# GateLoop attention and a maxout FFN on one core: the weights' conversion in four computing steps, joined output sums, constant biases, and new order lists

## The chip, the cores and the metric

The kernel runs on one core of one Trainium2 chip. The metric is the time of one execution on the device in microseconds (us). The engines are TensorE (PE in the profile, with its weight loads as PEld), VectorE (DVE), ScalarE (ACT), GpSimd (POOL) and SyncE (SP), which here only issues transfers. Each engine works off its own instructions in order.

## The reference

```python
batch, n_heads, seq, head_dim = (4, 8, 768, 48)           # q, k, v, a_re, a_im: float32
n_tokens, d_model, d_ff = (3072, 384, 768)                # w1, w2, w3, w_out: float64

mag = np.sqrt(a_re * a_re + a_im * a_im)
scale = np.minimum(mag, 0.999) / (mag + 1e-06)
a_re_n, a_im_n = (a_re * scale, a_im * scale)
for t in range(S):
    ar, ai = (a_re_n[:, :, t, :, None], a_im_n[:, :, t, :, None])
    new_re = ar * S_re - ai * S_im
    new_im = ar * S_im + ai * S_re
    kv = np.einsum('bhd,bhe->bhde', k[:, :, t], v[:, :, t])
    S_re, S_im = (new_re + kv, new_im)
    y[:, :, t] = np.einsum('bhd,bhde->bhe', q[:, :, t], S_re)
# y as (B*S, H*D) is x
h = np.maximum(np.maximum(x @ w1, x @ w2), x @ w3)
return (h @ w_out).astype(np.float32)
```

A linear recurrence whose state decays and turns by a complex gate at every step gives y; y is the input of a feed-forward layer that takes the largest of three products and multiplies it by a fourth matrix. The four weight matrices come as float64.

## The kernel before, in words

**Stages.** The 4 x 768 tokens are worked off in 12 groups g = 0 to 11, each of 128 positions of two batch rows, x and y. For each group the attention part works in chunks of 64 positions, and the feed-forward part takes the group's 256 tokens. Several groups are under way at once.

**Lists written out by hand.** `SCHEDULE` is one long list of words such as `Qcx:0`: a step's name (here with the batch row x) and its group. `run` issues the instructions of each word in the list's order, and the class `Bound` chains those of each engine, so that every engine keeps the list's order; waits between engines follow from the data. (All instructions pass through `Bound`, so the profile gives line 210 for nearly all of them and they are told apart by tiles.) `SLOTS` names, for each PSUM tile in order, which of four double banks it takes. `OTHER` names the words that run on another engine than the usual one: copies and magnitudes go to DVE in place of ACT, additions made by an accumulating transfer of POOL's queue go to DVE as an add.

**The steps.**

- `Lr`, `Li`, `Lk`, `Lq`, `Lv` load a_re, a_im, k, q, v on SP's queue; k, q and v with four transfers a word.
- Gates, on 128 x 768 tiles (two halves, `0` and `1`, in group 0): `sqr`, `sqi` (ACT squares), `add` (DVE), `lnL`, `expw`, `expe`, `relu`, `lne` (ACT), `Lnop` (adds lne's result to relu's, a transfer from group 1 on unless in `OTHER`), `abs`, `pw` or `addw` (a sum on PE, or from group 2 on an adding transfer or, in `OTHER`, DVE), `lnw`, `expL`, `mulai`, `mulw`, `stt`, `xor`, `half`, `atan`, `turn`. They end in the log magnitude `Ln` and the angle `w`.
- Angles: `cs` (running sums on PE), `t`, `nf`, `af`, `sa`, `sb` (sines), and `Cd`, a small adding transfer on POOL's queue that carries the last angle into the next group.
- Decays: `sums` and `F` (PE), `En`, `Ek`, `Eq`, `f0` to `f3` (ACT exponentials), `mk`, `mq`, `uk`, `uq`, `kEn` (DVE products).
- Scores: `tpk`, `tpq` (PE transposes), copies `Kc`, `Qc`; factors `Q1`, `Q2`, `KB`, `QB`, `QG` (DVE); `A`, `B` (PE) and picks into the masked tile: `g0` to `g3` (DVE), `b0`, `b1` (ACT).
- State and output: `dk` (PE), `h0` to `h3` (DVE); `y` (PE), copy `x`.
- Feed-forward: `U01`, `U11`, `U02`, `U12` (PE, 18 matmul instructions each) with `u..` (maximum with zero or with the other); sums `S1` to `S4` (DVE); products `P1` to `P7`, `Px`, `Py` (PE, a seven-product scheme); `r1` (ACT), `r6`, `r5`, `r7`, `r57`, `ox`, `oy` (DVE); stores `Dx`, `Dy` on SP's queue. Group 0 has forms of its own (`U..x`, `u..x`, `O`, `o`), six matmuls to each half product.

**The weights.** Twelve blocks i of doubles, 128 x 768 a block and 768 KB each, are loaded raw (`WLi`) and turned into float32 bit by bit: `Wa` (ACT) takes the high words, one in two, as floats, drops the sign and scales by 2^-112; `Wb` (DVE) limits; `Wc` (DVE) shifts left by 3; `We` (DVE) puts in the top bits of the low words; `Wf` (DVE) puts in the sign and writes the block. Blocks 0, 3 and 6 get the opposite sign. `Wg` adds the negated w1 to w2 or w3. `T`, `t`, `M`, `m` form the product of w1 and w_out, and `J` the differences of w_out that the seven products need. A raw block lies in a room that is free at that time (`ROOMS`).

**Set of functions.** `activation` loads ACT's table when a word's function belongs to another set than the loaded one; functions outside `SETS` count as being in every set.

**Tiles.** Tiles with two buffers come from pools (`ldx`, `nat2`, `un2`, `fp2`); `Ek` and `Eq` share the two buffers of tag `E`, `t` and `af` those of tag `t`.

Of the kernel before, what the change touches and what calls it, by code (L numbers as in the profile page):

```python
# [26 lines left out]
turn1:0 Lry:1 sqr:1 t1:0 WL11:0 Lkx:0 tx:0 nfx:0 Wa11:0 Wb10:0 csy:0 afx:0 sax:0 mkx:0 Wb11:0 Wc10:0 Lix:1 sbx:0
uqx:0 sqi:1 Lix:2 Wc11:0 Lky:0 tpqx:0 ty:0 add:1 f3x:0 f2x:0 ukx:0 Fy:0 Qcx:0 We10:0 Wf10:0 nfy:0 tpkx:0 We11:0
lnL:1 WL2:0 Q2x:0 kEnx:0 Eqy:0 expe:1 Eky:0 relu:1 xor:1 expw:1 QBx:0 Kcx:0 abs:1 T2:0 T0:0 t0:0 CL:0 KBx:0 WL1:0
Wa1:0 pw:1 Q1x:0 mky:0 Wb1:0 f0y:0 f1y:0 Wc1:0 t2:0 f2y:0 Wf11:0 lne:1 Lnop:1 Ax:0 g0x:0 Lry:2 g1x:0 We1:0 g2x:0  # L30
half:1 Lqy:0 Cdx:0 f3y:0 Liy:2 Lvx:0 mqy:0 Wa2:0 Wb2:0 lnw:1 expL:1 M0:0 mulw:1 Wc2:0 M1:0 mulai:1 dkx:0 Wf1:0
# [5 lines left out]
Wb7:0 Wg4:0 U11x:0 xor:2 By:0 dky:0 U02x:0 Lvx:1 b1y:0 h1y:0 b0y:0 QGy:0 yy:0 addw:2 lnw:2 expL:2 xy:0 U11y:0 Wg5:0
u02x:0 U02y:0 afx:1 half:2 u11x:0 Wc7:0 lne:2 We7:0 mulw:2 mulai:2 sbx:1 h2y:0 Z4:0 sax:1 h3y:0 stt:2 atan:2 Wf7:0
U12x:0 u12x:0 say:1 sby:1 Cdy:1 WL8:0 Cdx:1 turn:2 ukx:1 uqx:1 U01y:0 u01y:0 u11y:0 Wa8:0 U12y:0 csy:2 ty:2 u12y:0
csx:2 tpqx:1 tx:2 u02y:0 Qcx:1 nfy:2 Lnop:2 nfx:2 tpkx:1 Fy:1 kEnx:1 Wb8:0 Wc8:0 We8:0 Kcx:1 Wg7:0 Wf8:0 U21y:0  # L40
Wg8:0 KBx:1 f0y:1 u21y:0 Lky:1 Lqy:1 mky:1 afy:2 sumsx:2 dkx:1 Q1x:1 f1y:1 f2y:1 f3y:1 Enx:2 U21x:0 u21x:0 afx:2
U22y:0 u22y:0 Oy:0 Lqx:2 mqy:1 uky:1 uqy:1 tpqy:1 Ekx:2 Lix:3 Q2x:1 say:2 sby:2 sbx:2 sax:2 Eqx:2 h0x:1 h1x:1 QGx:1
h2x:1 oy:0 QBx:1 mkx:2 h3x:1 Qcy:1 Q1y:1 tpky:1 Kcy:1 Ax:1 g0x:1 Q2y:1 Liy:3 sqi:3 Fx:2 sumsy:2 g1x:1 g2x:1 U22x:0
Lrx:3 u22x:0 g3x:1 f3x:2 f2x:2 f1x:2 f0x:2 Lry:3 sqr:3 add:3 lnL:3 expe:3 Ay:1 relu:3 J3:0 g0y:1 g1y:1 mqx:2 g2y:1
Bx:1 KBy:1 kEny:1 lne:3 Ox:0 Eky:2 b1x:1 Eny:2 QBy:1 b0x:1 h0y:1 ukx:2 By:1 Eqy:2 yx:1 g3y:1 xx:1 b1y:1 Lqy:2 mqy:2
Lvx:2 ox:0 Lky:2 mky:2 b0y:1 tpkx:2 expw:3 Kcx:2 uqx:2 Lnop:3 uqy:2 tpqx:2 Qcx:2 QGy:1 dky:1 h1y:1 kEnx:2 sumsx:3
# [5 lines left out]
xx:2 By:2 u02:1 Ay:2 S1:1 nfy:3 relu:4 tx:3 expe:4 S2:1 expw:4 P5:1 P6:1 g0y:2 afy:3 say:3 sby:3 nfx:3 sbx:3 g1y:2
afx:3 sax:3 abs:4 dky:2 P1:1 Lqy:3 g2y:2 g3y:2 b1y:2 J4:0 QGy:2 P7:1 Px:1 P2:1 b0y:2 h0y:2 h1y:2 ukx:3 tpkx:3 lne:4
Lnop:4 r1:1 Liy:5 mky:3 h2y:2 h3y:2 S4:1 Kcx:3 uqx:3 yy:2 Lqx:4 kEnx:3 mqy:3 tpqx:3 Qcx:3 P3:1 r6:1 xy:2 Py:1 r5:1
r7:1 P4:1 Fy:3 uky:3 r57:1 f0y:3 f1y:3 xor:4 half:4 oy:1 ox:1 Q1x:3 addw:4 dkx:3 h1x:3 Lvy:3 f2y:3 f3y:3 h0y:3
h2x:3 sumsx:4 Ekx:4 h3x:3 lnw:4 QGx:3 expL:4 Eqx:4 Fx:4 KBx:3 U11:2 Dx:1 QBx:3 mulai:4 Q2x:3 f2x:4 Enx:4 u11:2
Cdy:3 Lkx:4 f1x:4 f0x:4 U01:2 uqy:3 f3x:4 mulw:4 stt:4 atan:4 tpky:3 Kcy:3 Ax:3 g0x:3 mqx:4 g1x:3 Bx:3 g2x:3 g3x:3
b1x:3 b0x:3 u01:2 Cdx:3 turn:4 U02:2 Lrx:5 u02:2 mkx:4 kEny:3 csy:4 csx:4 tx:4 nfx:4 ty:4 nfy:4 yx:3 xx:3 sumsy:4
KBy:3 Eqy:4 Eky:4 Lry:5 S3:2 Eny:4 sqr:5 dky:3 h1y:3 h2y:3 h3y:3 tpqy:3 Qcy:3 Q2y:3 Lix:5 sqi:5 Px:2 afy:4 add:5
lnL:5 expe:5 Dy:1 U12:2 u12:2 S1:2 Py:2 P7:2 Q1y:3 relu:5 lne:5 QBy:3 afx:4 P4:2 Ay:3 By:3 expw:5 S2:2 g0y:3 sbx:4  # L60
abs:5 g1y:3 sax:4 QGy:3 ukx:4 uqx:4 P6:2 P5:2 S4:2 g2y:3 g3y:3 P2:2 P1:2 Lqy:4 r1:2 Liy:6 mqy:4 b1y:3 P3:2 b0y:3
r6:2 r5:2 r7:2 tpkx:4 r57:2 ox:2 oy:2 kEnx:4 tpqx:4 yy:3 xy:3 Fy:4 say:4 Lky:4 sby:4 mky:4 uky:4 Lnop:5 Kcx:4 uqy:4
sumsx:5 xor:5 half:5 U11:3 KBx:4 addw:5 lnw:5 expL:5 mulw:5 Lqx:5 mulai:5 Cdx:4 h0x:4 f2y:4 stt:5 f3y:4 Ekx:5 f0y:4
Lkx:5 Dy:2 Dx:2 Qcx:4 Enx:5 Q1x:4 Cdy:4 u11:3 Eqx:5 QBx:4 mkx:5 Lry:6 QGx:4 Lvx:4 U01:3 Lix:6 atan:5 Q2x:4 u01:3
f1y:4 h0y:4 U02:3 Lrx:6 u02:3 sqr:6 dkx:4 h1x:4 sqi:6 h2x:4 h3x:4 Fx:5 f0x:5 f3x:5 add:6 f1x:5 f2x:5 Ax:4 g0x:4
Lqy:5 g1x:4 Bx:4 lnL:6 expe:6 g2x:4 g3x:4 U12:3 lne:6 b1x:4 tpky:4 turn:5 mqx:5 b0x:4 tpqy:4 Qcy:4 u12:3 Lvy:4
# [5 lines left out]
f1y:5 lnw:6 Lqx:6 h0y:5 u11:4 Q2x:5 expL:6 mulai:6 mulw:6 U01:4 u01:4 tpky:5 h0x:5 Eqx:6 Kcy:5 tpqy:5 stt:6 Ax:5
Lix:7 atan:6 g0x:5 Qcy:5 g1x:5 g2x:5 Bx:5 kEny:5 g3x:5 b0x:5 Q2y:5 U02:4 sqi:7 b1x:5 add:7 lnL:7 relu:7 expe:7
u02:4 U12:4 Fx:6 f2x:6 S3:4 f3x:6 half:6 turn:6 f0x:6 u12:4 Lvy:5 dky:5 h1y:5 Q1y:5 f1x:6 sumsy:6 dkx:5 Eny:6 csy:6
csx:6 h1x:5 mqx:6 S1:4 Dy:3 ty:6 nfy:6 S2:4 Eqy:6 Lqy:6 mqy:6 Eky:6 P1:4 KBy:5 tx:6 nfx:6 afx:6 lne:7 expw:7 afy:6
P7:4 abs:7 Lky:6 Ay:5 QBy:5 g0y:5 g1y:5 g2y:5 yx:5 g3y:5 addw:7 sbx:6 sax:6 ukx:6 uqx:6 By:5 say:6 P5:4 xx:5 P6:4
r1:4 r6:4 r5:4 lnw:7 xor:7 S4:4 half:7 Px:4 P2:4 b0y:5 Py:4 r7:4 P4:4 r57:4 P3:4 expL:7 mulw:7 QGy:5 oy:4 tpqx:6
tpkx:6 b1y:5 Lnop:7 mky:6 Qcx:6 Q1x:6 ox:4 Liy:8 kEnx:6 yy:5 sumsx:7 xy:5 Cdx:6 Enx:7 Fy:6 f2y:6 f0y:6 f3y:6
mulai:7 f1y:6 Eqx:7 QBx:6 QGx:6 Q2x:6 stt:7 Lqx:7 Ekx:7 Lix:8 U01:5 sqi:8 Lry:8 Cdy:6 Kcx:6 Lrx:8 Lvx:6 dkx:6 h1x:6
sby:6 mqx:7 h2x:6 h3x:6 uqy:6 uky:6 sqr:8 add:8 Dy:4 atan:7 turn:7 Ax:6 g0x:6 lnL:8 Lkx:7 expe:8 xor:8 g1x:6 relu:8  # L80
# [962 lines left out]
```

## Time and profile before

| | before |
|---|---|
| runs | 560.33, 556.86, 561.97 us; median 560.33 |
| profiled execution: span | 556.9 us, equal to the run of 556.86 |
| PE busy | 524.6 us (94%) |
| DVE busy | 490.4 us (88%), 770 instructions |
| ACT busy | 370.0 us (66%), 652 instructions |
| POOL busy | 74.4 us (13%) |
| DMA | 49.09 MB, mean 88 GB/s |

The span runs from the first to the last instruction. Busy time is the union of an engine's instructions; a matmul's end is modelled, and neighbours overlap. Rows of a view by groups read: line, engine, operation, out<-in by tile names, shape, count, then busy us, mean ns of one, and idle time before with what ended it.

### The profile page before, as it was taken

Reading aid. Unit: us, or ns where it says so; the run is one execution under the profiler, and the core shown is the slowest. Engines: PE = TensorE matmul, PEld = TensorE weight load, DVE = VectorE, ACT = ScalarE, POOL = GpSimd, SP = SyncE. Lnnn points to the kernel's source line nnn. Section 1 sums busy time; section 2 is a strip of 40 time slices with the busy share of each in tenths; the row PEclk is TensorE's granted clock in tenths of the full one; section 3 lists DMA queues with packets and bytes.
Section 4 is the critical chain, followed back from the end, with each engine's and each line's share of the span. In section 5 each row is a group of like instructions: output and inputs, shape, how many; then the busy total and the mean of one; then the engine's idle time right before and its main releaser. Section 6 shows DMA issues by size and latency. Waiting matters only on the chain.

```text
span 556.9 us, 22739 instructions
## 1 busy us (share of the span) xinstructions
PE 524.6 (94%) x10086; PEld 449.0 (81%) x10086; DVE 490.4 (88%) x770; ACT 370.0 (66%) x652; POOL 74.4 (13%) x117
## 2 busy tenths in 40 slices
PE   1669799989999999999999999999999999999997
...
DVE  5999999989998899999988897999999999886524
...
GB/s 218 287 191 156 206 154 102 78 105 123 18 108 109 21 123 77 48 63 92 68 115 82 33 61 121 110 88 50 58 126 31 32 88 82 10 31 2 7 25 29
DMA packets 142530, 49.09 MB, mean 88 GB/s; under 512 B 130528, under 2 KB 135648, under 8 KB 142432
## 3 DMA queue, kind: packets, MB, share of 16 engines
...
q14 instruction: 19, 0.16, 0.1%
...
## 4 chain that ended last, share of the span: by engine, by line
PE 84%; DVE 6%; DMA 4%; SPq 2%; issue 1%; ACT 1%; POOL 0%; DVEq 0%
PE up L210 34%; PE op L210 24%; PE y L210 7%; PE A L210 5%; PE tp L210 4%; PE dk L210 4%; PE sums L210 3%; PE cs L210 2%; SPq L210 2%; DMA xhx<-in_moe_w_out_dram 2%; PE F L210 2%; DVE xhx L210 1%; PE B L210 1%; DMA k<-in_k_dram 1%; DMA ar<-nf 1%
## 5 line engine op out<-in xcount | busy, mean ns | idle before, releaser
L210 PE MATMUL up<-xhx,w 128*128 128x256 f32 x792 | 177.4, 382 | 0.1
L210 PEld LDWEIGHTS up<-xhx,w 128*128 128x128 f32 x792 | 148.6, 190 | 21.5 <-PE B L210 0.3
L210 ACT ACT_TABLE_LOAD x45 | 57.7, 1283 | 1.5 <-PEq L1027 0.8
L210 ACT COPY atm<-B 32x128 f32<-32x128 f32 x96 | 24.5, 255 | 36.9 <-DVE atm L210 22.9
L210 PE MATMUL op<-wo,xhx 128*128 128x192 f32 (+1 forms) x220 | 48.5, 364 | 0.0
L210 DVE TENSOR_TENSOR Q<-Q,f 112x1024 f32<-112x1024 f32 (+1 forms) x48 | 45.4, 950 | 0.8 <-ACT Q L210 0.6
L210 ACT ACTIVATE f<-F 48x232 f32<-48x232 f32 x96 | 34.4, 359 | 13.2 <-PE F L210 5.4
L210 POOL DMA_DIRECT2D ar<-nf x40 | 34.2, 1280 | 65.3 <-DVE ar L210 54.7
L210 PE MATMUL y<-atm,vb 128*32 128x64 f32 x1152 | 39.4, 221 | 1.4 <-issue 1.1
L210 PEld LDWEIGHTS op<-wo,xhx 128*128 128x128 f32 x220 | 36.5, 190 | 4.3 <-DVE q L210 0.3
L210 POOL DMA_DIRECT2D Ln<-e x11 | 11.1, 1005 | 214.6 <-ACT e L210 53.9
L210 PE MATMUL y<-QG,g 112*32 112x64 f32 x1408 | 38.4, 219 | 0.9 <-issue 0.8
L210 PEld LDWEIGHTS y<-atm,vb 128*32 128x32 f32 x1152 | 32.5, 109 | 6.4 <-issue 3.6
L210 PEld LDWEIGHTS y<-QG,g 112*32 112x32 f32 x1408 | 34.8, 109 | 1.3 <-issue 1.0
L210 DVE TENSOR_TENSOR ot<-ot,op 128x192 f32<-128x192 f32 (+1 forms) x67 | 27.1, 413 | 9.0 <-PE op L210 4.3
L210 PE MATMUL op<-wo,strassen 128*128 128x192 f32 x176 | 33.0, 331 | 0.0
L210 PE MATMUL A<-Q,K 112*32 112x80 f32 x1536 | 31.6, 234 | 1.3 <-DVE Q L210 1.3
L210 DVE COPY_PREDICATED atm<-masko,A 128x256 f32<-128x256 uint8 x72 | 31.2, 435 | 1.6
L210 PE MATMUL op<-w,strassen 128*128 128x192 f32 x176 | 32.5, 329 | 0.0
L210 PEld LDWEIGHTS A<-Q,K 112*32 112x32 f32 x1536 | 27.2, 110 | 5.0 <-issue 1.9
L210 ACT COPY Q<-tp 112x1024 f32<-112x1024 f32 x23 | 23.3, 1013 | 10.3 <-PE tp L210 10.0
L210 ACT COPY ot<-op 128x192 f32<-128x192 f32 (+1 forms) x13 | 4.5, 342 | 38.2 <-PE op L210 38.2
...
## 6 DMA issues: line engine op xcount, KB each, us to landing
...
```

The lines of the kernel that those rows point to most:

```text
L210: ins = f(*a, **kw)
```

## The change

1. Conversion: `Wb` comes first, reads the high words from the raw block and limits them on both sides; `Wa` takes its result with a parametric rectifier, whose slope for negative inputs sets the bits that the shift turns into the sign; `Wf` is gone, and `We` writes the block.
2. Joined sums: `r5` and `r7` become one instruction `r75` over both halves, with the shared operand read twice.
3. Constant biases: three bias columns in SBUF become immediate numbers.
4. Tiles: the pools `ldx`, `nat2`, `un2`, `fp2` give way to fixed pairs, taken by c (x or y) or g; `Ek`, `Eq` and `En` have a pair each, `t` and `af` share one; `ot` is one tile for both rows.
5. `SCHEDULE`, `SLOTS` and `OTHER` are new throughout. The old list has 190 changes of PE's tile shape from step to step, the new one 187; 12 additions (`Lnop`, `addw`, `Wg8`) are in the new `OTHER`, 2 in the old.

```diff
-Lrx:0 Lix:0 sqi0:0 WL0:0 sqr0:0 xor0:0 add0:0 Wa0:0 Wb0:0 Wc0:0 We0:0 Liy:0 Wf0:0 lnL0:0 expw0:0 expe0:0 relu0:0
-lne0:0 Lnop0:0 Zf:0 Lry:0 sqi1:0 xor1:0 sqr1:0 WL3:0 abs0:0 add1:0 Wa3:0 half0:0 Wb3:0 Wc3:0 lnL1:0 expe1:0 expw1:0
-We3:0 lne1:0 relu1:0 Lnop1:0 Wf3:0 pw0:0 lnw0:0 expL0:0 mulai0:0 abs1:0 Lrx:1 half1:0 WL6:0 mulw0:0 Liy:1 Wa6:0
...
+Lrx:0 sqr0:0 Lix:0 sqi0:0 add0:0 lnL0:0 expe0:0 expw0:0 relu0:0 WL0:0 Wb0:0 lne0:0 Lry:0 sqr1:0 Wa0:0 Liy:0 Zf:0 sqi1:0
+Lry:1 WL3:0 Lqy:0 WL6:0 Lkx:0 WL9:0 Lix:1 WL10:0 Lqx:0 Lrx:1 Liy:1 Lnop0:0 abs0:0 Fx:0 sumsx:0 pw0:0 add1:0 Wc0:0 xor0:0
+Wb3:0 lnL1:0 f0x:0 expe1:0 expw1:0 relu1:0 lne1:0 Wa3:0 We0:0 Lnop1:0 half0:0 Wc3:0 Wb6:0 We3:0 xor1:0 f1x:0 abs1:0
...
-Zf:0 Zg:0 Wg8:0 xx:2 relu:4 afy:3 Kcy:3 xx:3 relu:5 xy:3 afx:5 addw:6 u01:4 afx:6 afy:6 abs:7 relu:8 Kcy:6 afy:7
-afx:7 relu:9 abs:9 u11:7 u01:7 afx:9 Kcx:9 xy:8 u11:8 Kcy:9 afy:10 abs:11 Kcx:10 Qcy:10 Kcy:11 Kcx:11 xy:11 u01:11
-u11:11
+Zf:0 Zg:0 afx:0 relu:1 Qcy:0 addw:2 Lnop:2 Wg8:0 u21y:0 xx:1 addw:3 relu:4 afy:3 afx:3 abs:4 Lnop:4 Kcx:3 u01:2 xx:3
+afy:4 afx:4 Qcx:4 u01:3 Kcy:4 xx:4 relu:6 xy:4 addw:6 u11:4 relu:7 afy:6 abs:7 addw:7 Lnop:7 u11:5 Lnop:8 Kcy:6 Qcy:6
+afx:7 Kcx:7 afy:8 Lnop:9 Qcx:8 xy:7 u01:7 afy:9 Qcx:9 xx:9 relu:11 afx:10 xy:9 Lnop:11 Kcx:10 addw:11 u01:9 Qcx:11
+Kcy:11 Qcy:11 Kcx:11 xx:11 xy:11 u11:11
...
-    LAST = float(np.array(0x0FEFFFFF, dtype=np.int32).view(np.float32))
+    LAST = float(np.array(0x47EFFFFF, dtype=np.int32).view(np.float32))
...
-    biases = const.tile([P, 4], FP, name="biases")
-    for i, b in enumerate((-0.5 * math.pi, LNMAX, math.exp(-LNMAX))):
-        dve.memset(biases[:, i:i + 1], b)
-    hpi, lnmax, least = (biases[:, i:i + 1] for i in range(3))
+    biases = const.tile([P, 1], FP, name="biases")
+    dve.memset(biases, 1.0)
...
+    kqs = {nm: two_of(nm, 2, 4, D) for nm in "kq"}
+    turned = {nm: two_of(nm, DM) for nm in ("t", "nf")}
+    css = two_of("CS", H, 2, D)
+    lns = two_of("Ln", W)
+    es = {nm: two_of(nm, DM) for nm in ("Ek", "Eq", "En")}
+    Ks, Qs = two_of("K", H, P), two_of("Q", 4 * H, 80)
+    ots = const.tile([P, C, DM], FP, name="ot")
...
-        if step == "a":
-            activation(out=ex.bitcast(FP), in_=high.bitcast(FP), func=AF.Abs, scale=2.0 ** -112)
-        elif step == "b":
-            dve.tensor_single_scalar(out=ex.bitcast(FP), in_=ex.bitcast(FP), scalar=LAST, op=OP.min)
+        if step == "b":
+            dve.tensor_scalar(out=ex.bitcast(FP), in0=high.bitcast(FP), scalar1=LAST, scalar2=-LAST, op0=OP.min,
+                              op1=OP.max)
+        elif step == "a":
+            activation(out=ex.bitcast(FP), in_=ex.bitcast(FP), func=AF.Prelu, alpha=-2.0 ** 32,
+                       scale=-2.0 ** -112 if i in (0, 3, 6) else 2.0 ** -112)
         elif step == "c":
-            if i in (0, 3, 6):
-                dve.tensor_scalar(out=ex, in0=ex, scalar1=3, scalar2=-0x80000000, op0=OP.logical_shift_left,
-                                  op1=OP.bitwise_or)
-            else:
-                dve.tensor_single_scalar(out=ex, in_=ex, scalar=3, op=OP.logical_shift_left)
+            dve.tensor_single_scalar(out=ex, in_=ex, scalar=3, op=OP.logical_shift_left)
         elif step == "e":
-            dve.scalar_tensor_tensor(out=ex, in0=low, scalar=29, in1=ex, op0=OP.logical_shift_right, op1=OP.bitwise_or)
-        elif step == "f":
-            dve.scalar_tensor_tensor(out=dst.bitcast(I32), in0=high, scalar=-0x80000000, in1=ex,
-                                     op0=OP.bitwise_and, op1=OP.bitwise_xor)
+            dve.scalar_tensor_tensor(out=dst.bitcast(I32), in0=low, scalar=29, in1=ex, op0=OP.logical_shift_right,
+                                     op1=OP.bitwise_or)
...
-                activation(out=e, in_=e, func=AF.Ln, scale=1e-6 * math.exp(-LNMAX), bias=least)
+                activation(out=e, in_=e, func=AF.Ln, scale=1e-6 * math.exp(-LNMAX), bias=math.exp(-LNMAX))
...
+                if name == "r75":
+                    two_ = ot.rearrange("p c n -> p (c n)")[:, NH:3 * NH].rearrange("p (u n) -> p u n", u=2)
+                    again = yl.rearrange("p (u n) -> p u n", u=1).to_broadcast([P, 2, NH])
+                    dve.tensor_tensor(out=two_, in0=again, in1=ps[:, 1, 0:DM].rearrange("p (u n) -> p u n", u=2), op=OP.add)
+                    return
```

More of the change, by code (lines that the diff above doesn't have):

```diff
@@ L27 @@
[L27 to L31, printed above, removed]
@@ L37 @@
[L37 to L41, printed above, removed]
@@ L42 @@
[L42 to L46, printed above, removed]
@@ L52 @@
[L52 to L56, printed above, removed]
@@ L57 @@
[L57 to L66, printed above, removed]
@@ L72 @@
[L72 to L80, printed above, removed]
-g2x:6 mkx:7 U11:5 KBx:6 u11:5 g3x:6 U12:5 u01:5 lne:8 U02:5 u12:5 S3:5 Lnop:8 u02:5 Bx:6 b0x:6 b1x:6 tpky:6 tpqy:6
@@ new lines @@
+Eqy:2 By:1 Ox:0 h1y:1 J3:0 Eky:2 b1y:1 lnL:3 relu:3 Eny:2 expe:3 expw:3 b0y:1 xor:3 mkx:2 uqx:2 ukx:2 h2y:1 QGy:1 mky:2
+uky:2 ox:0 abs:3 tpqx:2 tpkx:2 h3y:1 kEnx:2 addw:3 yy:1 Kcx:2 Qcx:2 xy:1 dkx:2 Fy:2 Q2x:2 Q1x:2 mqy:2 h0x:2 h1x:2 f0y:2
+f1y:2 f3y:2 lne:3 f2y:2 lnw:3 expL:3 uqy:2 QBx:2 half:3 U11:1 u11:1 J1:0 KBx:2 mulw:3 Lnop:3 tpky:2 tpqy:2 Ax:2 Kcy:2
+Qcy:2 Lvy:2 Liy:4 Lvy:3 Lry:4 Lrx:4 Lvx:3 Lqx:3 Lqy:3 Dx:0 U01:1 g0x:2 g1x:2 Q1y:2 g2x:2 g3x:2 h2x:2 Q2y:2 kEny:2 h3x:2
+Cdx:2 Cdy:2 sumsy:3 Bx:2 u01:1 Ay:2 Fx:3 h0y:2 mulai:3 g0y:2 g1y:2 b1x:2 b0x:2 sqr:4 Eny:3 g2y:2 stt:3 KBy:2 atan:3
@@ new lines @@
+Eky:3 g3y:2 U12:1 U02:1 QGx:2 sqi:4 Eqy:3 f1x:3 f0x:3 f3x:3 f2x:3 yx:2 QBy:2 u12:1 turn:3 add:4 J2:0 lnL:4 u02:1 S1:1
+xor:4 csx:3 csy:3 xx:2 tx:3 relu:4 nfx:3 sumsx:3 dky:2 ty:3 S2:1 Enx:3 expw:4 By:2 Ekx:3 Eqx:3 b1y:2 nfy:3 afx:3 h1y:2
+h2y:2 h3y:2 QGy:2 S3:1 P5:1 P6:1 Px:1 P1:1 P7:1 afy:3 expe:4 abs:4 say:3 sbx:3 b0y:2 sax:3 sby:3 r1:1 J4:0 addw:4 lne:4
+Dy:0 Lix:5 Lrx:5 Lry:5 Lkx:3 Liy:5 mqx:3 half:4 Cdx:3 S4:1 P2:1 P3:1 Py:1 yy:2 xy:2 uqx:3 r6:1 mkx:3 r75:1 ukx:3 mqy:3
+h0x:3 uqy:3 r57:1 tpkx:3 tpqy:3 tpqx:3 Lky:3 Kcx:3 kEnx:3 P4:1 Qcy:3 lnw:4 Qcx:3 Fy:3 dkx:3 expL:4 oy:1 Lnop:4 mky:3
```

202 lines of the change are left out of this document (112 added, 90 removed).

## The prediction

> **What bounds the kernel now.** I read four views in this order: the page, the table of busy time by stretches, the chain that ended last in order of time, and the groups of instructions by form. The page first: span, busy time, slices.
>
> ```profile
> span 556.9 us, 22739 instructions
> PE 524.6 (94%) x10086; PEld 449.0 (81%) x10086; DVE 490.4 (88%) x770; ACT 370.0 (66%) x652; POOL 74.4 (13%) x117
> PE   1669799989999999999999999999999999999997
> DVE  5999999989998899999988897999999999886524
> ```
>
> PE looks like the bound, but its first eight slices are loose while DVE is full from the second on. So I cut the span where it changes hands: at 9.38 (DVE begins to run without rest), 74.54 (step yy:0 starts on PE), 117.36 (yy:1 starts). The columns are stretch, length, then busy time and count of PE, PEld, DVE, ACT, POOL, the clock, DMA share and GB/s.
>
> ```profile
> 9.38:74.54 65.16, 49.36 (x762) 32.72 (x762) 64.58 (x100) 61.38 (x109) 21.00 (x31) 0.90 0.89 212
> 74.54:117.36 42.82, 41.48 (x881) 33.41 (x880) 41.78 (x66) 36.74 (x66) 6.40 (x7) 1.00 0.58 105
> 117.36:556.90 439.54, 433.76 (x8447) 382.83 (x8444) 381.11 (x594) 267.81 (x471) 40.01 (x48) 1.00 0.35 66
> 100.00:180.00 80.00, 78.36 (x1788) 66.25 (x1790) 76.16 (x120) 56.31 (x103) 10.04 (x12) 1.00 0.51 94
> 300.00:500.00 200.00, 199.86 (x4069) 176.35 (x4068) 184.13 (x287) 127.81 (x232) 19.99 (x24) 1.00 0.35 67
> ```
>
> DVE is busy 64.6 of 65.2 us and then 41.8 of 42.8; after 117.36 PE is busy 433.8 of 439.5. The time is therefore **DVE's list up to about yy:1, then PE's list to the end**. The chain agrees: DVE pieces up to 74, PE pieces behind (start, length, what).
>
> ```profile
> 61.89 0.95 DVE L L210
> ...
> 73.58 0.86 DVE ai L210
> 75.09 1.15 PE y L210 x64
> 76.80 7.12 PE up L210 x60
> ...
> 126.08 1.04 PE tp L210 x28
> ...
> 132.36 1.24 PE A L210 x64
> 133.90 4.08 PE up L210 x18
> 137.98 1.73 PE y L210 x112
> 143.79 1.45 PE cs L210 x16
> 149.57 1.07 PE dk L210 x57
> ...
> 164.17 7.97 PE up L210 x36
> 204.31 11.85 PE up L210 x54
> ```
>
> These give PE's price of each step: U 3.98 (one alone 4.08, two 7.97, three 11.85), y 1.73, A 1.24, a pair tpk and tpq 1.04, a pair cs 1.45, dk 1.0, and so on. Summed along the old list they give 434.5 us of PE work from yy:1 to the end; the table above has 433.8 busy there.
>
> **The change, part by part.** Durations of the operations that come, go or move:
>
> ```profile
> L210 DVE SCALAR_TENSOR_TENSOR w<-w,xhx 128x768 int32<-128x768 int32 x3 | 2.9, 952 | 0.0
> L210 DVE SCALAR_TENSOR_TENSOR w<-w,ai 128x768 f32<-128x768 f32 x11 | 10.5, 952 | 0.1
> L210 DVE TENSOR_SCALAR xhx<-xhx 128x768 f32<-128x768 f32 x12 | 7.5, 621 | 2.8 <-ACT xhx L210 2.7
> L210 ACT ACTIVATE xhx<-w 128x768 f32<-128x768 f32 x4 | 3.6, 912 | 2.5 <-DMA w<-in_moe_w_dram 2.5
> L210 DVE TENSOR_TENSOR w<-w,L 128x768 f32<-128x768 f32 x11 | 10.5, 951 | 0.0
> L210 POOL DMA_DIRECT2D Ln<-e x11 | 11.1, 1005 | 214.6 <-ACT e L210 53.9 <-DVE QB L210 50.8 <-ACT xhx L210 34.8
> L210 DVE COPY Q<-tp 112x1024 f32<-112x1024 f32 x1 | 1.2, 1225 | 0.5 <-PE tp L210 0.5
> L210 DVE TENSOR_SCALAR Ln<-L 128x768 f32<-128x768 f32 x4 | 2.2, 551 | 0.0
> L210 DVE TENSOR_TENSOR ot<-ot,op 128x192 f32<-128x192 f32 x46 | 16.1, 351 | 5.9 <-ACT ot L210 3.7 <-PE op L210 1.3
> L210 DVE TENSOR_TENSOR ot<-ot,op 128x384 f32<-128x384 f32 x21 | 11.1, 549 | 3.1 <-PE op L210 3.0
> L210 ACT ACTIVATE e<-e,biases 128x768 f32<-128x768 f32 x7 | 6.6, 938 | 0.0
> L210 ACT ACTIVATE e<-e 128x768 f32<-128x768 f32 x4 | 3.4, 844 | 0.1
> L210 ACT ACT_TABLE_LOAD x45 | 57.7, 1283 | 1.5 <-PEq L1027 0.8
> ```
>
> On a full DVE neighbours overlap, as two starts 0.47 us apart show at a duration of 0.55:
>
> ```profile
> 28.19 0.55 DVE L210 SCALAR_TENSOR_TENSOR nf<-t,cs 128x384 f32<-128x384 f32 x1
> 28.66 0.55 DVE L210 TENSOR_SCALAR xhx<-xhx 128x768 f32<-128x768 f32 x1
> ```
>
> So I charge each DVE instruction its duration less 0.075.
>
> *Conversion.* Step f is gone: 12 x (0.952 - 0.075) = 10.5 us off DVE, every one ahead of yy:1. Step b now reads the high words out of the raw doubles, every second word, instead of a dense tile. The trace has no one-source DVE instruction on such an input. Lower bound 0.55 (28.66 above; the mean of 621 holds a few lengthened ones), so nothing is lost; upper bound the 0.952 of the full-length instructions, +0.40 each, +4.8 in all. I take the lower: step f's row reads that same alternate word at 952 ns, just like the dense `w<-w,ai` at 952, so the gap in the input costs nothing there. [...] Step a's ACT work goes from strided (912) to dense (844), 12 x 0.07 = 0.8 off ACT.
>
> *Joined sums.* r5 and r7 (2 x 0.276) become one r75 of 384 columns (0.474): 11 x 0.08 = 0.9 off DVE in late stages, where PE covers it: nothing.
>
> *Constant biases.* 938 against 844: 0.09 off some 40 ACT instructions, 3.8 us; ACT rests 72 of the 200 us from 300 on, so nothing there.
>
> *Adding transfers and other moved steps.* Ten more adds go from POOL's queue to DVE (2 before, 12 now, weights' Wg8 in both), 10 x 0.88 = 8.8 us. Ahead of yy:1 the new list has addw:2 and Lnop:2 (0.88 each), relu:1 (0.48), afx:0 (0.28), Qcy:0 (1.15), xx:1 (0.48), u21y:0 (0.34) new on DVE: together 4.5. Behind yy:1 the new list has 384.5 us of DVE work for 370.2, 14.3 more, with copies of K, Q and x among it; DVE rests 58 of those 440 us, so I book it at nothing, and without that cover it costs up to 14 us. What was queued behind these adds on POOL, the carry transfers Cd, gets free earlier. Each Lnop on DVE now stops DVE until ACT's lne is done; behind it stand products and picks for A, y and dk.
>
> *Lists and tiles.* Fixed tiles keep the same two buffers, and Ek and Eq no longer share theirs; nothing. Changes of PE's tile shape fall from 190 to 187; two U together take 7.97 against 2 x 4.08, so a change costs 0.19 and three save 0.6. On SP the q and k loads of stage 0 now stand ahead of some weight blocks, and DVE itself, no longer ACT, waits for a block to land.
>
> *Sum.* Ahead of yy:1 the old list has 104.7 us of DVE work. It ended at 117.3 (116.74 and 0.55, the sum into the carried state that yy:1 needs), since DVE began late and rested a little:
>
> ```profile
> 115.05 1.22 DVE L210 TENSOR_TENSOR QG<-Q,f 112x1024 f32<-112x1024 f32 x1
> 116.74 0.55 DVE L210 TENSOR_TENSOR g<-g,dk 112x384 f32<-112x384 f32 x1 [0.48 <-PE dk L210]
> ```
>
> The new list has 104.7 - 10.5 + 4.5 - 0.5 (some moved past) = 98.2 behind QGy:1, the last that yy:1 needs: -6.5. PE's rest is 435.2, +0.7. The tile changes give -0.6, mostly inside that rest already, so I count none. DVE's first conversion step starts 0.9 earlier, as it needn't wait for step a. Against that stands ACT: in the old list ACT's work ahead of mulai0 (9.0) equals DVE's (9.1); in the new one it is 11.0 against 7.9. DVE will wait for ACT in the first 35 us; bounds 0 and the whole 3.1, I take half, 1.5. By yy:1 that makes 556.9 - 6.5 + 0.7 - 0.9 + 1.5 = 551.7, with the 5 us of PE waits behind yy:1 (439.5 less 434.5) kept. In the new order an earlier step is later: Oy:0 needs u22y:0, with 80.0 us of DVE work ahead of it and 455.3 of PE from Oy:0 on, 535.3 together, where yy:1 has 533.4. The old list's u22y:0 ended 12.1 after the work ahead of it:
>
> ```profile
> 93.30 0.42 DVE L210 TENSOR_TENSOR hT<-hT,up 128x256 f32<-128x256 f32 x1 [0.16 <-PE up L210]
> ```
>
> (93.7 for 81.6.) 80.0 + 12.1 + 455.3 + 5.0 - 0.9 + 1.5 = **553.0**, for an execution like the profiled one.
>
> The profiled execution is the fastest of the three shown (556.86, 560.33, 561.97); the median lies 3.4 higher, and nothing in one trace says how far the new kernel's median will lie above its best, from 0 to 3.4. Fewer landings of adding transfers are waited for, so I add 1.0: **554.0**, 1.1% under the median.
>
> **Rivals.**
>
> *The head stays as long* (ACT or a landing bounds it, or step b runs at 0.95). For it: ACT is busy 61.4 of 65.2, so DVE's relief soon meets it; DVE's step b stands in front of everything while blocks land. Against: the alternate-word rows. Price: +4.8 for step b, or the 6.5 not gained: 558 to 559.5, with the median's 1.0 some 559.5.
>
> *More falls away.* The 5 us of waits behind yy:1 shrink too, and ACT isn't met: 553.0 - 4 - 1.5 = 547.5. For it: 300 to 500 shows PE idle just 0.14 us, so an order with almost no waits exists.
>
> *DVE starves PE in stages 1 to 5 (slower).* Place: 100 to 180, where DVE rests 3.8 of 80 us and stages 3 and 4 bring it two of the adds, three copies of K or Q and other moved steps, net 6 us; Lnop holds DVE until lne, with the picks for y behind it. It decides (slower by 1%) once PE's idle time behind yy:1 exceeds 5 + 3.9 + 5.6 = 14.5 us. If each of the ten adds lets PE wait 1.5 us: 553 + 15 = 568. Against: DVE work ahead plus PE work behind is 533.6 at dkx:3 and 527.7 at Ax:5, under the head's 535.3.
>
> *The new activation function isn't in ACT's loaded table.* Two loads around each of 12 steps a, 24 x 1.28 = 31 us of ACT, nearly full there: at least 575. Against: 45 loads are exactly the list's 44 changes of set and the first, so the fillers (absolute value, copy) cause none. [...]
>
> **How the numbers follow.** Forecast 0.50 (own range 549 to 558, four fifths of it at least 1% faster); head as long 0.20; more falls away 0.10; starved 0.14; tables 0.06. One per cent (5.6 us, about what a measurement here can tell) sets the bounds 554.7 and 565.9. Faster: 0.40 + 0.10 = 0.50. Slower: 0.14 + 0.06, and 0.02 from the tail of the second case: 0.22. Same: 0.10 + 0.18 = 0.28. The range runs from 545 to 564; it leaves out the tables and most of the starved case.
>
> **What would show it.** Right: DVE full from 8.5 us; step b at 0.55; yy:1 starting at 111 to 114; PE idle about 5 us behind it; 49 table loads (the new list has four more changes of set, 5 us of ACT). Wrong: step b near 0.9, DVE gaps put down to ACT or landings in the first 40 us above 5 us, or PE idle of over 10 us between 115 and 300.

## The result: 565.7 us, 1.0% slower, and the profile after

The changed kernel takes 565.68 us (median of four runs, 564.95 to 567.12); the kernel before, run beside it on the same chip, 560.81. The ratio is 1.010, with a 95% interval of 1.006 to 1.014. The forecast was 554.0, 1.1% faster.

The page of the changed kernel (span, busy times, then the 40 slices of PE, DVE and of the granted clock):

```profile
span 565.0 us, 22654 instructions
PE 527.3 (93%) x10086; PEld 449.6 (80%) x10086; DVE 495.2 (88%) x769; ACT 359.5 (64%) x642; POOL 65.0 (12%) x107
PE   3669689999999999999999999999999999999997
DVE  3899999999999999989989898999999999797423
PEclk9779999999999999999999999999999999999999
```

The span is 8.1 us longer than before's 556.9; the medians differ by 4.9, since the profiled executions are single ones: before's was a good one, this one (567.12) is the slowest of its four.

First the arithmetic, in groups by form of the changed kernel (step b on two of its kinds of block, step a, step c, and the table loads):

```profile
L202 DVE TENSOR_SCALAR xhx<-w 128x768 f32<-128x768 f32 x4 | 2.5, 613 | 4.5 <-DMA w<-in_moe_w_dram 4.5
L202 DVE TENSOR_SCALAR xhx<-strassen 128x768 f32<-128x768 f32 x3 | 1.7, 555 | 0.0
L202 ACT ACTIVATE xhx<-xhx 128x768 f32<-128x768 f32 x12 | 10.1, 841 | 4.4 <-DVE xhx L202 4.3
L202 DVE TENSOR_SCALAR xhx<-xhx 128x768 int32<-128x768 int32 x12 | 9.1, 756 | 0.0
L202 ACT ACT_TABLE_LOAD x49 | 62.9, 1283 | 1.6 <-PEq L1028 0.8
```

Step b takes 0.55 to 0.61 us on alternate words, as on a dense tile (0.55 and 0.62 in the kernel before); step f is gone; the new function costs no table load beyond the list's own (49 loads). Behind the bars stands what is new: 4.5 us of DVE idle before step b, for a landing, and 4.3 of ACT before step a, for DVE.

The busy times by stretches, of the kernel before (first four rows) and of the changed one (columns as in the prediction):

```profile
10.00:20.00 10.00, 7.80 (x68) 3.45 (x72) 9.63 (x18) 9.25 (x20) 6.37 (x13) 1.00 1.09 335
40.00:60.00 20.00, 19.35 (x283) 12.19 (x282) 19.93 (x30) 18.92 (x28) 10.40 (x13) 1.00 0.79 169
60.00:80.00 20.00, 16.12 (x415) 13.78 (x416) 19.86 (x32) 18.06 (x37) 7.54 (x9) 1.00 0.89 182
80.00:100.00 20.00, 19.89 (x286) 16.27 (x285) 19.57 (x30) 17.74 (x32) 1.63 (x2) 1.00 0.55 91
```

```profile
10.00:20.00 10.00, 7.12 (x62) 3.96 (x58) 5.74 (x11) 7.93 (x19) 5.24 (x14) 1.00 0.95 262
40.00:60.00 20.00, 16.09 (x172) 9.49 (x171) 19.93 (x29) 17.05 (x29) 9.15 (x13) 1.00 0.90 197
80.00:100.00 20.00, 19.76 (x370) 16.71 (x371) 19.32 (x34) 15.96 (x29) 1.12 (x2) 1.00 0.57 97
118.22:565.00 446.78, 437.11 (x8464) 382.75 (x8460) 389.88 (x599) 261.48 (x466) 34.59 (x41) 1.00 0.29 58
```

DVE is busy 5.7 us of 10 to 20 where it was 9.6; PE then gets 16.1 us of work in 40 to 60 instead of 19.4. From yy:1 (118.22) to the end PE rests 9.7 us, where it rested 5.8; none of that lies right behind yy:1 (up to 180 us PE rests 0.1 of 61.8). DVE's waits in the first 120 us (total, times, longest; first the two long ones of the kernel before, then those of the changed one), and the places on the changed kernel's DVE timeline:

```profile
DVE xhx L210 <- ACT xhx L210: 2.7, 1, 2.7
DVE ai L210 <- ACT L L210: 2.6, 1, 2.6
```

```profile
DVE xhx L202 <- DMA w<-in_moe_w_dram: 4.5, 3, 2.4
DVE L L202 <- ACT L L202: 4.1, 2, 3.1
DVE xhx L202 <- DMA wo<-in_moe_w_dram: 1.2, 1, 1.2
DVE Ln L202 <- ACT e L202: 0.9, 1, 0.9
```

```profile
10.65 0.56 DVE L202 CUSTOM_DVE_ANT_0 L<-L,e 128x384 f32<-128x384 f32 x1 [1.00 <-ACT L L202]
...
14.63 0.75 DVE L202 TENSOR_SCALAR xhx<-w 128x768 f32<-128x768 f32 x1 [2.44 <-DMA w<-in_moe_w_dram]
...
18.61 0.56 DVE L202 TENSOR_SCALAR xhx<-wo 128x768 f32<-128x768 f32 x1 [1.16 <-DMA wo<-in_moe_w_dram]
```

A landing that used to stop ACT now stops DVE, with all that is queued behind it. SP's queue shows why blocks 3 (`w`), 6 (`wo`) are late:

```profile
4.90 2.39 SPq L202 DMA_DIRECT2D ar<-in_a_re_dram  x1
7.33 0.70 SPq L202 DMA_DIRECT2D w<-in_moe_w_dram  x1
8.08 2.68 SPq L202 DMA_DIRECT2D q<-in_q_dram  x4
10.81 0.60 SPq L202 DMA_DIRECT2D wo<-in_moe_w_dram  x1
11.46 4.42 SPq L202 DMA_DIRECT2D k<-in_k_dram  x4
```

A gate load of group 1, q (2.7 us to issue) and k (4.4) stand between the blocks, which take 0.6 to 0.7 each. Behind yy:1 PE's waits are these, at the changed kernel's longest places:

```profile
PE y L202 <- issue: 2.5, 2, 1.3
PE cs L202 <- DVE g L202: 1.0, 1, 1.0
PE op L202 <- DVE ot L202: 0.6, 1, 0.6
PE y L202 <- DVE g L202: 0.4, 1, 0.4
```

The kernel before has only the first kind there, 1.9 us.

### The profile page after: what moved, and what is told of

It reads as the page before. It is cut to its first block, busy times and chain, and to the rows that moved or that the text cites. A ratio compares the mean times of both kernels' runs of the same rounds, so it can differ in the third digit from the quotient of the medians.

```text
span 565.0 us, 22654 instructions
## 1 busy us (share of the span) xinstructions
PE 527.3 (93%) x10086; PEld 449.6 (80%) x10086; DVE 495.2 (88%) x769; ACT 359.5 (64%) x642; POOL 65.0 (12%) x107
## 4 chain that ended last, share of the span: by engine, by line
PE 69%; DVE 16%; DMA 5%; SPq 4%; issue 4%; ACT 1%; POOL 0%; DVEq 0%; ACTq 0%
PE up L202 27%; PE op L202 20%; PE y L202 5%; SPq L202 4%; PE A L202 4%; PE tp L202 3%; DVE w L202 3%; PE dk L202 3%; DVE atm L202 2%; PE cs L202 2%; PE sums L202 2%; DVE g L202 1%; DVE xhx L202 1%; DMA w<-in_moe_w_dram 1%; DMA wo<-in_moe_w_dram 1%
## 5 line engine op out<-in xcount | busy, mean ns | idle before, releaser
L202 ACT ACTIVATE xhx<-up 128x768 f32<-128x768 f32 x15 | 12.2, 812 | 53.3 <-PE up L202 53.3
L202 DVE TENSOR_TENSOR ot<-ot,op 128x384 f32<-128x384 f32 (+1 forms) x56 | 25.8, 464 | 13.4 <-PE op L202 7.1
L202 PEld LDWEIGHTS op<-w,strassen 128*128 128x128 f32 x176 | 29.0, 190 | 2.3 <-DVE strassen L202 0.3
L202 PEld LDWEIGHTS op<-wo,strassen 128*128 128x128 f32 x176 | 28.7, 190 | 0.7 <-DVE strassen L202 0.2
```

What stands on the lines that cost most here:

```text
L202: ins = f(*a, **kw)
```

## The experiments

Ratios are to the kernel before on the same chip, with 95% intervals; the changed kernel has 1.010 (1.006 to 1.014). Theory 1 of the start: the arithmetic gains and the new lists lose it. Its rivals, and what took their place, stand with the runs.

### Arithmetic under the old order

```diff
 all lists of before;  code of the changed kernel
-... Wa3 ... Wb3 Wc3 ... We3 ... Wf3 ... r5 ... r7
+... Wb3 ... Wa3     ... Wc3 ... We3 ...         r75
```

> The changed kernel's arithmetic (conversion without step f, joined sums, constant biases, fixed tiles) under the old order lists, slots and engine assignment; step b stands where a stood, a where b stood, c where e stood, e where f stood. Theory 1 (the arithmetic gains, the new lists lose it): DVE's work ahead of yy:1 falls by 10.5 us against before, ACT's by less than 1, so some of the 10.5 turns into DVE waits; yy:1 starts 4 to 8 us earlier (109 to 113), PE's waits behind it stay near 5, and the median is 552 to 556, where before has 560.8. Rival (the head is bounded by ACT or by landings in any order, so the relief of DVE is worth nothing): DVE idle in the head rises by about 10 us, yy:1 still near 117, median 559 to 562.

569.8 us, 1.022 (1.017 to 1.027): outside of both. Here Lkx:2 (the load of k of group 2) stands ahead of mkx:1, so that with fixed tiles k of group 2 replaces that of group 1 (mkx:1 waits for that later load and works on it), and ox:11 stands ahead of r75:11. Its waits are those of neither order; the next runs keep the old tiles.

```diff
 kernel before, with the new conversion only:
-... Wa3 ... Wb3 Wc3 ... We3 ... Wf3 ...
+... Wb3 ... Wa3     ... Wc3 ... We3 ...     (conv_only; conv_bias: also bias=<number>)
+... Wb3 Wa3 ...     Wc3 ... We3 ...         (a_kept: a, c, e where they were)
```

> The kernel before with its old lists, tiles, sums and biases; only the conversion is the new one of four steps (b where a stood in the list, a where b stood, c where e stood, e where f stood). Theory A (the shorter conversion gains in DVE's list, and the new order of the changed kernel loses it): DVE's 10.5 us fewer ahead of yy:1 bring yy:1 to 109 to 113, PE's waits behind it stay near 5, time 551 to 556. Theory B (once the conversion takes some 2.5 us of DVE for a block that takes some 3.7 us to land, landings and ACT bound the head under any order): DVE idle before 40 us rises to 6 us or more, yy:1 at 115 to 117, time 557 to 560.

> The same as the kernel before with the new conversion, and also the three bias columns replaced by numbers. It takes about 0.09 us off each of some 40 ACT instructions, about ten of them ahead of 40 us. Theory B, in which ACT is one of the bounds of the head: 0.5 to 1.5 us less than with the conversion alone. Theory A: the same within 0.5 us.

> The kernel before with the new conversion, and every word of its list where it was: step a keeps its place on ACT, c and e theirs on DVE, b goes ahead of a by up to 8 DVE words as far as its buffer is free (0 to 2 words for most blocks), f is gone. Theory C (the second crossing costs what step f gains: ACT, whose order is now exactly that of before, waits for b, DVE for a): ACT waits 5 us or more on DVE's b, DVE on ACT's a, yy:1 no earlier than before, 560 to 568. Rival (the run with the conversion alone was slow only because a and c stood too late in the list): 552 to 557.

Measured: 1.014 (1.009 to 1.019), 1.015 (1.010 to 1.021) and 1.014 (1.009 to 1.018), 566 to 568.5 us, all slower than before although DVE has 10 us less to do. Theory A falls, and so does theory B's level; the biases do nothing that can be seen. ACT's waits in a_kept up to 118 us, where ACT's order is exactly that of before:

```profile
ACT xhx L207 <- DVE xhx L207: 7.7, 6, 3.4
```

Six times ACT stands still for DVE's step b. Before, step a waited only for the landing. The conversion of four steps is shorter, but goes DVE, ACT, DVE where the old one went ACT, DVE, as theory C says. It isn't the only thing that takes the gain: in a_kept DVE also waits 5.6 us once for a block to land, and PE's stops without a wait (more below) add up to 7.7 us in conv_only and 8.0 in a_kept, for 1.9 in the kernel before. No run parts these.

```diff
 changed kernel, with the old conversion:
-Wb3 ... Wa3 ... Wc3 ... We3
+Wa3 ... Wb3 ... Wc3 ... We3 Wf3
```

> The changed kernel with its new lists, but with the old conversion of five steps (a where b stands, b where a stands, c, then e and f together where e stands). DVE gets 12 x 0.88 = 10.5 us more work ahead of yy:1. As the prediction reckoned (DVE is the bound of the head throughout): about 10 us more than the changed kernel, 574 to 577. Theory B (landings and ACT bound the head of the new order up to about 40 us, so that step f of blocks 0, 3, 6, 9 and 10 runs in DVE's idle time): only the later blocks' steps cost, 7 x 0.88 and less, 568 to 572.

1.039 (1.034 to 1.043), 581.3 us: some 16 us over the changed kernel, more than either said; the first row of DVE's waits up to 120 us shows why:

```profile
DVE xhx L204 <- ACT xhx L204: 7.6, 3, 3.7
```

Step b now waits for ACT's step a at a place made for the other direction. So each mixture is slower than the kernel before; old_lists and five_steps are slower than the changed kernel too, the three with the old lists and tiles (1.014 to 1.015) can't be told from it (1.010). The two parts of the change have no prices that add up.

### Loads in the head

```diff
 SP, changed kernel:  Lrx Lix WL0 Lry Liy Lry:1 WL3 Lqy WL6 Lkx WL9 Lix:1 WL10 Lqx Lrx:1 Liy:1
+blocks_first:        Lrx Lix WL0 Lry Liy WL3 WL6 WL9 WL10 Lkx Lqx Lry:1 Lix:1 Lqy Lrx:1 Liy:1
+due_order:           Lrx Lix WL0 Lry Liy WL3 WL6 WL9 Lkx WL10 Lrx:1 Lry:1 Lix:1 Liy:1 Lqx WL11 | WL1 WL2 Lqy ...
+need_order:          Lrx Lix WL0 Lry Liy WL3 WL6 WL9 Lkx WL10 Lrx:1 Lry:1 Lix:1 Liy:1 Lqx Lqy
```

> The changed kernel with five loads of its SP list (Lkx:0, Lqx:0, Lry:1, Lix:1, Lqy:0) moved behind the weight blocks 3, 6, 9 and 10; nothing else. Theory 1a (the head's loss is DVE waiting for weight blocks that stand behind other loads on SP): the 4.8 us of DVE idle time in front of Wb3, Wb6 and Wb1 shrink to under 2, DVE's lag at We3 falls from 13.1 to about 10, and the median falls by 2 to 4 us from the changed kernel's 565.7, to 562 to 564. Rival (the transfers share one rate that is full in the head, or ACT's turns with DVE bound it): the idle time comes back in front of other steps, lag at u22y:0 still near 17.5, median 565 to 567.

1.012 (1.008 to 1.016), no gain. The 4.7 us of waits for blocks 3, 6 and 1 are gone, but DVE then waits 2.2 us at add:1 for ACT, whose squares wait for the gate loads now behind k and q.

> The changed kernel with the first 27 loads of its list in the order in which their data are needed: blocks 3, 6 and 9 right behind the gates of group 0, then Lkx:0, block 10, the four gate loads of group 1, Lqx:0, blocks 11, 1 and 2, and only then Lqy:0 and Lvx:0 (used at 36 and 62 us). Nothing else. Theory D (SP's queue is the bound of the head: a word of q, k or v takes some 3 us to issue there, a block or a gate load some 0.6; with blocks first, blocks landed early but the gate loads of group 1 stood behind k and q): no DVE wait on a landing behind Wb0, none of 2.2 us in front of add:1, lag at Wb11 under 11 (13.1 in the changed kernel), yy:1 2 to 3 us earlier, time 562 to 564. Rival (the turns between ACT and DVE bound the head): DVE's waits move to ACT, lag at u22y:0 stays near 17, 565 to 566.

> The order of loads by need and the two late moves (half:7 with Cdx:6, Cdy:6, and P4:11) together. If head and late waits are separate causes, the gains add: the late moves alone took 1.9 us, so 560 to 562, level with before. Rival (what the head gains is waited away later, since DVE is late behind yy:1 as well): 563 to 564.

1.031 (1.028 to 1.033) and 1.029 (1.026 to 1.032). That order is no order of need: block 11 goes into the room of w1 ahead of step e of block 0, and DVE waits for it:

```profile
DVE w L204 <- DMA w<-in_moe_w_out_dram: 15.0, 1, 15.0
```

These two say nothing on theory D, but give a price: 15 us of DVE standstill at 12.6 us cost 12 to 13 us at the end (by ratios and by medians).

> The changed kernel with its first 16 loads in the order of need (blocks 3, 6 and 9 behind the gates of group 0, then Lkx:0, block 10, the four gate loads of group 1, Lqx:0 and Lqy:0). In the run before that had block 11 among them, block 11 went into the room of w1 ahead of step e of block 0, which then waited 15 us for its landing; here block 11 and all later loads keep their places. Theory D (order on SP's queue bounds the head): no DVE wait for a landing behind Wb0, none above 0.5 us in front of add:1, lag at Wb11 10 to 11 (13.1 in the changed kernel), yy:1 2 to 3 us earlier, 562 to 564. Rival (the turns between ACT and DVE bound it): lag at u22y:0 stays near 17, 565 to 566.

1.009 (1.006 to 1.012). Of the waits for blocks 3 and 6 nothing is left; DVE's lag (end of a step less the work ahead of it) at Wb11 falls from 13.1 to 11.4. But yy:1 starts at 117.6 instead of 118.2: of 1.7 us won, 0.6 arrive. Some of it stayed where the granted clock fell (need_order, two stretches of 3 us):

```profile
57.00:60.00 3.00, 1.91 (x38) 1.66 (x39) 3.00 (x4) 2.20 (x6) 0.00 (x0) 0.74 1.15 316
60.00:63.00 3.00, 3.00 (x86) 2.31 (x86) 2.35 (x4) 2.12 (x4) 0.00 (x0) 0.69 0.68 105
```

There the pair of cs steps takes 2.75 us, where the changed kernel, which has 1.00 from 40 us on, takes 1.52. PE's rest by itself doesn't explain the difference: it is busy 3.41 of 6 us in 54 to 60 here, and 3.41 of 6 in 57 to 63 in the changed kernel, at the same steps.

### Late waits

```diff
 late_two:   -mulai:7 half:7 Cdx:6 Cdy:6 ... ox:11 P4:11
             +xor:7 half:7 Cdx:6 Cdy:6 ...   P4:11 ox:11
 need_late:  both of need_order and late_two, and Dx:11 ahead of oy:11
```

> The changed kernel with two moves in the list: half:7, Cdx:6 and Cdy:6 go from behind mulai:7 to right behind xor:7, and P4:11 goes ahead of ox:11. Theory 3 (some late waits are single places where the new order puts a word too late): the wait of 1.0 us in front of csy:7 and that of 0.65 us in front of P4:11 vanish, and the median falls by 1 to 2 us to about 564. Rival (PE's late waits come from DVE being behind as a whole, so one that is removed is met again a little later): median 565 to 566, and the totals of start and remaining PE work at yy:9 stay near 558.

> The same order of loads and the late moves (half:7 with Cdx:6 and Cdy:6 behind xor:7, P4:11 ahead of ox:11, Dx:11 ahead of oy:11). If head and late places are separate causes the gains add: 559.5 to 562, level with before. Rival (what the head gains is waited away behind yy:1): 563 to 564, as with the late moves alone.

late_two: 1.009 (1.006 to 1.013); need_late: 565.1 us, 1.005 (1.004 to 1.007). In late_two the rows for cs and op are gone from PE's waits; its median is 1.8 below that of the changed kernel, but the ratios don't tell them apart. With the loads as well half of the loss seems to be gone, but only just: the two intervals still touch, and the median lies 0.6 below that of the changed kernel. No version here beats the kernel before.

```diff
 OTHER:  adds_pool   - Lnop:2,4,7,8,9,11  addw:2,3,7,11
         adds_late   - Lnop:4,7,8,9,11  addw:3,7,11
         copies_act  - Kcx:3 Qcx:4 Kcy:4 Qcy:6 Kcx:7 Qcx:8 Qcx:9 Qcx:11 Qcy:11
 slim_u: uk, uq  [:, 0:8 heads]  ->  [:, 0:1]  for g >= 3
```

> The changed kernel with the ten adds Lnop:2,4,7,8,9,11 and addw:2,3,7,11 back on POOL's queue as adding transfers; addw:6 and Wg8 stay on DVE as before. Theory 2 (the adds on DVE make PE wait behind yy:1): PE's waits behind yy:1 fall from 11.6 us to about 6, DVE's work ahead of Oy:0 falls by 1.8; median 558 to 561. [...]

> The changed kernel with only the eight later adds back on POOL's queue: Lnop:4,7,8,9,11 and addw:3,7,11; Lnop:2 and addw:2 stay on DVE. In the run with all ten back, 13.4 us were lost by yy:1, where mulw:2 waited 7.9 us, and 2.2 us behind it. Theory 2 (the adds cost DVE time that PE waits for behind yy:1): 2 to 5 us less than the changed kernel, 561 to 564. Rival (DVE has the room, and the order counts on the adds being short): 566 to 569.

> The changed kernel with nine copies of K and Q (Kcx:3, Qcx:4, Kcy:4, Qcy:6, Kcx:7, Qcx:8, Qcx:9, Qcx:11, Qcy:11) back on ACT: about 10 us less DVE work behind yy:1, 9 us more on ACT, which rests there. Theory 2b (DVE as a whole is late behind yy:1): PE's waits fall from 11.6 to 6 to 9, 561 to 564. Rival (the order counts on these copies running on DVE, right behind the transposes): 565 to 570.

> The changed kernel with the 36 products uk and uq of groups 3 to 11 worked out for one head of eight only, everything else and all waits kept: some 29 us less DVE work behind yy:1. Theory 2b: PE's waits behind yy:1 fall from 11.6 to about 5 (what is left is the end and the waits for nothing in front of y), 557 to 560. Rival (single places in the order, the carry into csy:7 and the end): 563 to 565.

1.040 (1.037 to 1.044), 1.013 (1.010 to 1.017), 1.017 (1.012 to 1.021) and 1.011 (1.007 to 1.015). The ten adds are no burden: back on POOL they cost 16 us (in the kernel before, an adding transfer `Ln<-e` lands 4.7 us after its issue, median of 11; the add on DVE takes 0.95), half of it at one place: DVE stands at mulw:2 for ACT, and ACT ahead of that for what the profile puts down to a carry transfer, which has the adds ahead of it on POOL's queue (adds_pool, first rows of DVE's and of ACT's waits up to 120 us; then slim_u behind 118 us):

```profile
DVE w L201 <- ACT L L201: 7.9, 1, 7.9
```

```profile
ACT hT L201 <- DMA ar<-nf: 8.4, 1, 8.4
```

```profile
118.00:561.30 443.30, 435.71 (x8456) 382.10 (x8444) 365.76 (x598) 260.91 (x466) 34.52 (x41) 1.00 0.29 59
```

slim_u takes 24 us off DVE behind yy:1 (365.8 for 389.9), and PE still rests 7.6 us for 9.7. So most of the late waits don't come from DVE having too much to do; theory 2, by which some 5 would be left, falls in all four runs. Of the 9.7 us, 1.6 are two single places (csy:7, P4:11), 2.5 are stops that the profile puts down to no wait; the rest is spread in pieces under 0.5, and what makes them isn't settled.

### What DVE's relief is worth by itself

```diff
 before_slim_f:   step f  [:, :, 0:8] only, e writes dst      (lists of before)
 before_slim_fa:  also step a  [:, :, 0:8], blocks other than 0 and 3
 after_slim_a:    step a  [:, :, 0:8]                        (lists of the changed kernel)
```

> The kernel before, its lists untouched, with step f worked out for 8 of the columns of each row of a block only (step e writes the block): DVE's work falls by about 10 us ahead of yy:1 and nothing else changes. The prediction's step (DVE's list is the bound there, a microsecond off it is a microsecond): yy:1 at 108 to 110, 548 to 552. Theory E (ACT is the second bound, busy 61.4 of 65.2 us in the head, so DVE's relief turns into waits for ACT): yy:1 at 113 to 116, 554 to 558.

> The same, and step a of the blocks other than 0 and 3 worked out on ACT for 8 columns only: about 6 us less ACT work ahead of yy:1. (Step c shifts the other way, so that the left out columns stay finite.) Theory E: ACT's relief lets DVE's through, yy:1 3 to 6 us earlier than with step f alone. The prediction's step: no more than with step f alone, within 1 us.

> The changed kernel with step a worked out on ACT for 8 columns only (step c shifts the other way): about 7 us less ACT work ahead of yy:1, and the way from b over a to c shorter by 0.6 us a block; all waits are kept. Theory E and the second crossing: yy:1 2 to 5 us earlier, 561 to 564. If landings alone bound the head: 565 to 566.

before_slim_f: 563.5 us, 1.004 (1.0005 to 1.007). With 10 us less on DVE and no new crossing the kernel isn't faster. before_slim_fa: 1.000 (0.997 to 1.002), yy:1 at 117.2, as before. after_slim_a: 1.011 (1.007 to 1.015); yy:1 is 1.7 us earlier, and the end isn't. So neither DVE alone nor DVE with ACT bounds the stretch. Two stretches of the kernel before, then the same of before_slim_f, then two pieces of its PE timeline:

```profile
66.00:69.00 3.00, 2.84 (x76) 2.54 (x76) 3.00 (x7) 2.94 (x6) 0.00 (x0) 1.00 1.20 221
69.00:72.00 3.00, 2.18 (x59) 2.00 (x62) 3.00 (x5) 2.61 (x6) 0.90 (x1) 1.00 0.67 123
```

```profile
66.00:69.00 3.00, 0.74 (x30) 0.62 (x29) 1.03 (x2) 2.94 (x6) 0.00 (x0) 1.00 0.93 156
69.00:72.00 3.00, 3.00 (x17) 3.00 (x16) 2.88 (x6) 0.90 (x3) 0.90 (x1) 0.54 0.39 71
```

```profile
68.26 0.75 PE L210 MATMUL A<-Q,K 112*32 112x80 f32 x29 [2.42 <-issue]
68.94 4.57 PE L210 MATMUL up<-xT,w 128*128 128x128 f32 x24
...
118.94 0.33 PE L210 MATMUL y<-QG,g 112*32 112x64 f32 x9 [3.08 <-issue]
```

Relieved, DVE brings PE its data sooner (A starts at 64.95 us, in the kernel before at 66.16). PE stops 2.4 us in the middle of a step without any wait that the profile shows, and DVE waits for PE (up to 118 us 4.5 us for A and 3.2 for U; in the kernel before 0.2 for U). The granted clock falls to 0.54 in 69 to 72 us, and 24 matmuls of a U step take 4.57 us, where the kernel before has 1.60 + 1.58. A second stop, 3.1 us, follows at yx:1, and yy:1 starts at 124.5. The lower clock alone doesn't eat the gain: of the twelve runs the one with the highest mean clock (0.988) took 561.84, the profiled one (0.979) 564.19.

before_slim_fa has the same stop at the same instruction, and the same long U step, though its yy:1 comes at 117.2:

```profile
65.40 0.75 PE L210 MATMUL A<-Q,K 112*32 112x80 f32 x29 [2.35 <-issue]
66.08 4.57 PE L210 MATMUL up<-xT,w 128*128 128x128 f32 x24
```

There the balance can be drawn. From 30 to 118 us PE's waits for DVE fall from 5.1 us (kernel before) to 0.3; in their place stand 3.5 us of stops without a wait (2.3 in A, 1.2 in dk) and 1.4 us of a longer U step. So what DVE's relief gave PE in this execution, PE lost again.

What the stops are can be read in part from the DMA rows. The page has a queue for instructions (kernel before; transfers, MB, share):

```profile
q8 instruction: 79, 1.29, 1.0%
```

That is 16 KB a transfer; if all of them are for PE, an estimated 64 bytes for each of its 20172 matmuls and weight loads. From 40 us on the kernel before, the changed one, before_slim_f, before_slim_fa, conv_only and a_kept have twenty stops of over 0.75 us without a wait, and nineteen of them end 2.2 to 2.6 us after such a transfer starts (the transfer at the stop above starts at 63.1, and PE goes on at 65.40). The author reads this as a PE that has used up its instructions and waits for the next ones; no run changes the number of instructions, so it isn't shown.

In before_slim_f the granted clock was 1.00 in the 3 us in which PE was busy 0.74 of 3, 0.54 in the 3 us behind them, 0.89 in the next 3 and 1.00 after those; before_slim_fa has 1.00 (PE busy 0.65 of 3), 0.54, 0.90 and 1.00. The stops themselves lasted 2.42 and 2.35 us. By what rule the clock is granted, no run shows.

## Why the prediction was wrong

**The bound up to yy:1: wrong, the main failure.** "DVE's list up to about yy:1" was read from DVE's full rows. But PE, too, is nearly full from 40 us on in the kernel before (19.35, 16.12 and 19.89 of 20, above); the row from 9.38 to 74.54 averaged this with PE's loose first 30 us. From 40 us on some 5 us were to be had at most. A microsecond taken off DVE is worth a microsecond only where PE and ACT have room: before_slim_f puts 10 us of relief at nothing, and in before_slim_fa stops of PE and a lower clock take back the 4.8 us by which PE waits less for DVE.

**Work ahead of yy:1, -6.5.** The durations were right (step b at 0.55, f gone), and the sum of DVE's work was right. What it is worth was not.

**Conversion starts 0.9 earlier, ACT wait +1.5.** Together these terms are +0.6; measured +5.4. DVE's waits in the head are 4.5 + 1.2 for landings and 4.1 + 0.9 for ACT; before had 2.7 + 2.6, all for ACT. By u22y:0 (97.12 and 0.41, with 80.0 of work ahead) DVE lies 17.5 behind its work, not 12.7 as the sum has it. The text says that "DVE itself, no longer ACT, waits for a block to land" and gives it no price; by SP's rows it could have had one. The waits alone make up the difference (10.7 less 5.3). The text's own sign of being wrong, over 5 us of DVE gaps for ACT or landings in the first 40 us, came.

```profile
97.12 0.41 DVE L202 TENSOR_TENSOR hT<-hT,up 128x256 f32<-128x256 f32 x1
```

**Oy:0.** Forecast 548.0 before PE's late waits (553.0 less 5.0), measured 96.69 + 455.3 = 552.0 (PE's timeline), 4.0 of the 12.0 us between 553.0 and 565.0:

```profile
96.69 1.56 PE L202 MATMUL op<-wo,ot 128*128 128x384 f32 x4
```

**PE waits kept at 5.0: wrong by the other 8.0.** Behind Oy:0 565.0 - 552.0 = 13.0 are lost. The 5.0 had been counted behind yy:1, not Oy:0; behind yy:1 alone 11.6 are lost (446.8 less the 435.2 of PE work), 9.7 of them as rest. The late rest of DVE (58 us of 440) was taken to cover any order. It covers most of the amounts (slim_u takes 24 us off DVE and gives PE 2.1), not single places. Where some 5.6 us of the late rest come from stays open.

**Adds, biases, joined sums, tile changes at nothing; the table rival.** The runs with the adds, the copies and the biases agree, and the 49 loads refute the table rival; joined sums and tile changes have no run of their own. The rival of a starved PE had neither its mechanism (the adds) nor its place (stages 1 to 5) right: up to 180 us PE rests 0.1 us behind yy:1, and its losses lie later.

**Median.** The profiled execution isn't the run of 556.86, though the table and the prediction equate them. The changed kernel's span of 565.0 belongs to a time of 567.12, so 2.1 lie outside the span; with the 1.7 that lie outside it in most runs of the kernel before, before's profiled one took about 558.6 (an estimate).

Of the rivals, "the head stays as long" is nearest: ACT's turn and a landing take DVE's place, as it says. It stops at 559.5, since it kept the 5 us of late waits.
